# Softmax transposes taken from TensorE: through DRAM by GpSimd's queue, then VectorE

## The chip, the cores and the metric

The kernel runs on one core of one Trainium2 chip. The metric is the device time of one execution in microseconds. Runs of the kernel before took 885.91 to 886.01 us, with a median of 885.98 us (three runs).

The five engines of a core are TensorE (PE, with its weight loads as PEld), VectorE (DVE), ScalarE (ACT), GpSimd (POOL) and SyncE (SP), which in this kernel only issues DMAs. Each engine runs its own list of instructions in the order in which the program gave them to it, and waits at an instruction until what it needs is there.

## The reference

The program computes sliding-window attention, and two feed-forward layers on its output, all in float32:

```python
def _attn_ref(q, k, v):                      # each [4, 8, 576, 64]
    scores = scale * np.matmul(q, k.transpose(0, 1, 3, 2))
    rel = pos[:, None] - pos[None, :]
    mask = (rel >= 0) & (rel < 64)
    scores = np.where(mask, scores, -1000000000.0)
    scores = scores - np.max(scores, axis=-1, keepdims=True)
    attn = np.exp(scores)
    attn = attn / (np.sum(attn, axis=-1, keepdims=True) + 1e-09)
    return np.matmul(attn, v)

# layer 1, on x [2304, 512]: weights [512, 2048] and [2048, 512]
h = x @ w_in;  r = np.maximum(h, 0.0);  x = (r * r) @ w_out
# layer 2, same shapes
h = x @ w_in
P = a[0] + a[1] * h + a[2] * h**2 + a[3] * h**3
Q = 1.0 + abs(b[0]) * abs(h) + abs(b[1]) * h**2
out = (P / (Q + 1e-06)) @ w_out
```

## The kernel before

The 2304 tokens are cut into blocks of 512, 512, 512, 512 and 256. For each block of layer 1, sixteen steps j multiply a slice of the hidden layer (`h_mm`, L619: twelve matmuls of 128x512, three for each of four pieces of the inner dimension, because every float32 factor is split into a high and a low part of type float32r) and add its product into four accumulators in PSUM (`out_mm`, L638). Between the two, `mid1` applies the activation on ACT and DVE and ends with a subtraction on DVE (L692), which `out_mm` waits for. When a block ends, `evac1` copies the accumulators out (L705 to L707) to DRAM. These matmuls are the "big matmuls" of this text. Layer 2 does the same with `mid2` and L640.

The attention is computed for sub-blocks of 128 tokens, index i from 0 to 17. The first block's four sub-blocks stand ahead of everything. The sub-blocks of block n+1 are computed while PE works on layer 1 of block n, as short visits put between the big matmuls. A sub-block has these slots:

- `q` and `k`: the transposes of q and k. Up to index 11 PE does them; from 12 (`NPE`) on DVE does, as 32x32 transposes (L463, L485), of data that SP's DMAs have put through DRAM so that the 32x32 squares lie in the right places.
- `s` (`slot_s`): the scores, 16 small products in float32 (L525) into two PSUM banks, one for each half `gl` of the sub-block. `softmax` follows for each half: `top` on DVE (L542: mask, and the row's least negative score), `exp` on ACT (L547), `norm` and `mul` on DVE (L551 to L555), in a tile `sm` of 128 rows by 4x128 keys.
- `p` (`slot_p`), one for each half: PE transposes the four 128x128 parts of `sm` into a PSUM bank (L568), and ACT or DVE copies that to a tile `pT` (L573).
- `x` (`slot_x`): the values, 16 small products of `pT` with v (L585), whose result `split_x` splits into the high and low part of layer 1's input (L602, L603).
- `sx` (`slot_sx`): the scores of i and the values of i-1 in one visit of PE. Within a block all scores but the first are taken in this way.

While that goes on, `convert` (L399 to L419) also turns layer 2's weights into high and low parts on ACT and DVE, and SP moves them to DRAM.

The order of everything is made by a planner (class `Plan`): each piece of work is an item with the engines that could do it, a duration in ns, and a due time. `run` always takes the item that can start first, and among those the one that is due first, on a model of five resources ("pe", "act", "dve", "pool", "dma"). An item can start when those it depends on have ended plus a gap: 2000 ns after a DMA, 150 to 200 after most others. On the chip the planned times are gone: only each engine's order is left. `softmax`'s tiles take turns in a ring of two buffers (`sm0`, `sm1`); layer 2's `mid2` uses the same ring for its tile `ab`.

Of the kernel before, what the change touches and what calls it, by code (L numbers as in the profile page):

```python
# [9 lines left out]
F32 = mybir.dt.float32  # L10
F32R = mybir.dt.float32r
U32 = mybir.dt.uint32
ACTF = mybir.ActivationFunctionType
ALU = mybir.AluOpType
# [25 lines left out]
class Item:  # L40
    def __init__(self, engines, emit, due):
        self.engines, self.emit, self.due = engines, emit, due
        self.deps, self.users = {}, []
        self.end = None


class Plan:
# [42 lines left out]
    def run(self):  # L90
        for it in reversed(self.items):
            least = min(it.engines.values())
            for u in it.users:
                d = u.due - least - 150
                it.due = d if it.due is None else min(it.due, d)
            assert it.due is not None
        left = {it: len(it.deps) for it in self.items}
        free = dict.fromkeys(self.ENGINES, 0)
        open_ = {e: [] for e in self.ENGINES}
        order = []  # L100

        def opened(it):
            it.ready = {}
            for e in it.engines:
                it.ready[e] = max([d.end + self.gap(d.on, e) for d in it.deps], default=0)
                open_[e].append(it)

        for it in self.items:
            if not left[it]:
                opened(it)  # L110
        while len(order) < len(self.items):
            best = None
            for e in self.ENGINES:
                for it in open_[e]:
                    start = max(free[e], it.ready[e])
                    key = (start, it.due)
                    if best is None or key < best[0]:
                        best = (key, it, e)
            (start, _), it, e = best
            it.on, it.end = e, start + it.engines[e]  # L120
            free[e] = it.end
            for x in it.engines:
                open_[x].remove(it)
            order.append(it)
            for u in it.users:
                left[u] -= 1
                if not left[u]:
                    opened(u)
        for it in order:
            it.emit(it.on)  # L130
# [6 lines left out]
def dve(n, fast=False, ptr=0):  # L137
    return 68 + 1.042 * n / (2 if fast else 1) + 61 * ptr
# [3 lines left out]
def window_attention__moe_relu2__moe_rational_kernel(  # L142
# [21 lines left out]
    nc = tc.nc  # L164
# [8 lines left out]
    NSUB = NT // 128  # L173
    blocks = [(t0, min(512, NT - t0)) for t0 in range(0, NT, 512)]
    NB = len(blocks)
    orders = (list(range(NB)), list(range(NB - 2)) + [NB - 1, NB - 2])
    NS0 = blocks[0][1] // 128
    NPE = sum(n for _, n in blocks[:3]) // 128
    scale = 1.0 / float(D) ** 0.5

    ctx.enter_context(tc.manual_schedule())
    sb = ctx.enter_context(tc.tile_pool(name="sb", bufs=1))
    dram = ctx.enter_context(tc.tile_pool(name="dram", bufs=1, space=bass.MemoryType.DRAM))
    psum = ctx.enter_context(tc.tile_pool(name="psum", bufs=1, space=bass.MemoryType.PSUM))

    V, A, P, T = nc.vector, nc.scalar, nc.gpsimd, nc.tensor
    plan = Plan()
# [6 lines left out]
    SMALL = [("cb", 2), ("coef", 6), ("na", 4), ("b1", 1)] + [(f"{x}{i}", 4) for x in ("nm", "su", "rs") for i in range(4)]  # L194
    TAGS = ([("ident", [128, 128], F32), ("mask", [128, 2, 128], F32)] +
            [(f"kT{i}", [128, HP, W + 128], F32) for i in range(2)] + [(x, [128, n], F32) for x, n in SMALL] +
            [("pad", [128, 224], F32)] +
            [(f"wi{x}{j}", [128, DM], F32R) for j in range(NF) for x in "hl"] +
            [(f"wo{j}", [128, KT, 2, 2, 128], F32R) for j in range(NF // 2)] +
            [(f"x{x}{i}", [128, 4, KT, 128], F32R) for i in range(2) for x in "hl"] +  # L200
# [10 lines left out]
    mask = sb.tile([128, 2, 128], F32, tag="mask", name="mask")  # L211
# [19 lines left out]

    sq_d = {x: dram.tile([128, HP, (NSUB - NPE) * 4, 32], F32, name=f"{x}_squares_d") for x in "kq"}


    turn = {}

    def buf(place, shape, dtype=F32, pool=sb, view=None):

        if not isinstance(place, str):
            n = turn.get(place, 0)  # L240
            turn[place] = n + 1
            place = place[n % len(place)]

        def make():
            t = pool.tile(shape, dtype, tag=place, name=place)
            return view(t) if view else t

        return Buf(plan, place, make)

    def ring(name, n):  # L250
        return tuple(f"{name}{i}" for i in range(n))
# [3 lines left out]

    ALL_PS = ("t0", "h0", "t1", "h1", "acc0", "acc1", "acc2", "acc3")
    LD, RAW, CV = ring("ld", 6), ring("raw", 3), (0, 1, 2)
    KTP, QTP, SM, PT = ring("kT", 2), ring("qT", 2), ring("sm", 2), ring("pT", 2)
    shared = {}

    def part(place, tag, shape, dtype, view, gen=0):
# [51 lines left out]

    nat = {}

    def load(dst, pieces, size, slow=1, reads=(), due=None):
        def emit(_):
            for o, i in pieces():
                nc.sync.dma_start(out=o, in_=i)
        return plan.add({"dma": size / 360 * slow}, emit, reads, [dst], due)  # L320

    def toks(t0, n):
        done = 0
# [13 lines left out]
    def squares(nm, c, last, token):  # L337


        src = {"k": k, "q": q}[nm]  # L340
        pieces = list(toks(NPE * 128, NT - NPE * 128))
        b = sq_b[nm, c, last] = Buf(plan, f"{nm}_squares{c}{last}", None)
# [111 lines left out]
    def ps_buf():  # L454
        return buf(ps_places[0], [128, 512], F32, psum, cols(128))

    qT, kT, sm, pT = {}, {}, {}, {}
# [76 lines left out]
    def softmax(i, gl, ps):  # L534
        t = early(NF - 5 - i, gl, 128) if i < NS0 else buf(SM, [128, 4, 128])
        sm[i, gl] = t
        kind = int((2 * i + gl) % GPB == 0)
        nm, su, rs = (buf(ring(x, 4), [128, 4]) for x in ("nm", "su", "rs"))

        def top(_):  # L540
            for c in range(4):
                V.tensor_tensor_reduce(out=t.t[:, c, :], in0=ps.t[:, c, :], in1=mask[:, kind, :], scale=-scale,  # L542
                                       scalar=-NEG, op0=ALU.add, op1=ALU.min, accum_out=nm.t[:, c:c + 1])

        def exp(_):
            for c in range(4):
                A.activation(out=t.t[:, c, :], in_=t.t[:, c, :], func=ACTF.Exp, scale=-1.0, bias=nm.t[:, c:c + 1],  # L547
                             accum_out=su.t[:, c:c + 1])

        def norm(_):  # L550
            V.tensor_scalar(out=rs.t, in0=su.t, scalar1=1e-9, scalar2=None, op0=ALU.add)  # L551
            V.reciprocal(out=rs.t, in_=rs.t)

        def mul(e):
            (P if e == "pool" else V).tensor_tensor(out=t.t, in0=t.t, in1=rs.t.unsqueeze(2).to_broadcast([128, 4, 128]),  # L555
                                                    op=ALU.mult)

        plan.add({"dve": 850}, top, [ps], [t, nm])
        plan.add({"act": 1550}, exp, [nm, t], [t, su])
        plan.add({"dve": 350}, norm, [su], [rs])  # L560
        plan.add({"pool": 1400} if i < NS0 else {"dve": 690}, mul, [rs, t], [t])

    def slot_p(i, n, due):
        src, ps = sm[i, n], ps_buf()

        def tr(_):
            for c in range(4):
                T.transpose(ps.t[:, c, :], src.t[:, c, :], ident)  # L568

        plan.add({"pe": 430}, tr, [src], [ps], due)  # L570
        t = pT[i, n] = early(NF - 5 - i, 2 + n, 128) if i < NS0 else buf(PT, [128, 4, 128])
        plan.add({"act": act(512, True), "dve": dve(512)}, lambda e: (
            A.copy(out=t.t, in_=ps.t) if e == "act" else V.tensor_copy(t.t, ps.t)), [ps], [t])  # L573

    def slot_x(i, due, ps=None):
        joined = ps is not None
        ps = ps or ps_buf()
        vg = [nat["v", 2 * i + gl] for gl in range(2)]
        pt = [pT[i, n] for n in range(2)]

        def mm(_):
            for hp in range(HP):
                for gl in range(2):
                    for e in range(2):
                        T.matmul(  # L585
                            out=ps.t[e * 64:(e + 1) * 64, hp, gl * W:(gl + 1) * W],
                            lhsT=vg[gl].t[:, 2 * hp + e, :],
                            rhs=pt[gl].t[:, hp, (e ^ gl) * 64:((e ^ gl) + 1) * 64],
                            start=True, stop=True,
                        )  # L590

        if joined:
            return vg + pt, [ps], mm
        plan.add({"pe": 1250}, mm, vg + pt, [ps], due)
        split_x(i, ps)
# [173 lines left out]
    def slots_of(first, last):  # L769

        o = []
        for i in range(first, last):
            o += [("sx" if i > first else "s", i)]
            o += [("q", i + 1)] if i + 1 < NSUB else []
            o += [("p", i, 0)]
            o += [("k", i + 1)] if i + 1 < NSUB else []
            o += [("p", i, 1)]
        return o + [("x", last - 1)]
# [25 lines left out]
    for l in range(2):  # L804
# [4 lines left out]
        for s in range(len(steps) + 1):  # L809
            lag = LAGS[l][0] if s < len(steps) - NF else LAGS[l][1]  # L810
            if s < len(steps):
                bi, j = steps[s]
                due = due_h(l, bi, j)
                if l == 0 and j == 0 and bi + 1 < NB:
                    f = blocks[bi + 1][0] // 128
# [12 lines left out]
                hp = h_mm(l, bi, j, due)  # L828
                gs[s] = (mid1 if l == 0 else mid2)(bi, j, hp)
                if l == 0 and NF - 2 <= s < NF - 2 + 4 * HP:  # L830
                    z, c = divmod(s - NF + 2, 2 * HP)
# [11 lines left out]
            if l == 0 and s < len(steps):  # L843
                while slots and slots[0][1] < due_h(0, bi, j + 1):
                    x, d = slots.pop(0)
# [43 lines left out]
```

## Time and profile before

| | |
|---|---|
| median of 3 runs | 885.98 us |
| the profiled execution's own time | 890.21 us |
| its span in the profile | 888.4 us |
| TensorE's mean granted clock | 0.996 of full speed |
| TensorE busy | 870.5 us, 98% |
| VectorE busy | 674.3 us, 76% |
| ScalarE busy | 561.0 us, 63% |
| GpSimd busy | 11.5 us, 1% |
| DMA, moved in all | 113.64 MB |

The profile shows one execution, by the hardware's own profiler. "Busy" is the time in which an engine had an instruction in work. Matmuls overlap each other, so that PE's busy time says that it was never without work, and not that the work could not be done in less; where a visit's price is needed it is read from the starts of the matmuls around it. A wait is put down to the instruction that released it.

### The profile page before, as it was taken

Reading aid. Unit: us, or ns where it says so; the run is one execution under the profiler, and the core shown is the slowest. Engines: PE = TensorE matmul, PEld = TensorE weight load, DVE = VectorE, ACT = ScalarE, POOL = GpSimd, SP = SyncE. Lnnn points to the kernel's source line nnn. Section 1 sums busy time; section 2 is a strip of 40 time slices with the busy share of each in tenths; the row PEclk is TensorE's granted clock in tenths of the full one; section 3 lists DMA queues with packets and bytes.
Section 4 is the critical chain, followed back from the end, with each engine's and each line's share of the span. In section 5 each row is a group of like instructions: output and inputs, shape, how many; then the busy total and the mean of one; then the engine's idle time right before and its main releaser. Section 6 shows DMA issues by size and latency. Waiting matters only on the chain.

```text
span 888.4 us, 14088 instructions
## 1 busy us (share of the span) xinstructions
PE 870.5 (98%) x5152; PEld 726.5 (82%) x5152; DVE 674.3 (76%) x1435; ACT 561.0 (63%) x1172; POOL 11.5 (1%) x25
## 2 busy tenths in 40 slices
PE   7799999999999999999999999999999999999998
PEld 6678788888878888888899888888888888988886
DVE  6999995666466676754421899999999999999994
ACT  6778774656456554535444766676667667888764
POOL 4000000000000000000000000000000000000000
PEclk9999999999999999999999999999999999999999
DMA  9686662688855453633189910210011002100001
GB/s 230 187 243 199 188 192 84 200 219 220 223 179 184 147 184 141 238 134 126 49 313 372 361 45 0 96 48 1 1 47 48 1 1 94 49 1 24 1 1 48
DMA packets 152998, 113.64 MB, mean 128 GB/s; under 512 B 92769, under 2 KB 131681, under 8 KB 150881
## 3 DMA queue, kind: packets, MB, share of 16 engines
q1 hardware_dynamic: 152928, 112.75, 41.0%
q8 instruction: 40, 0.66, 0.3%
q14 instruction: 30, 0.24, 0.1%
HBM read 81.79 MB, written 34.08 MB: 130 GB/s over the span
## 4 chain that ended last, share of the span: by engine, by line
PE 88%; DVE 6%; DMA 3%; ACT 2%; issue 1%; SPq 0%; POOLq 0%; POOL 0%; ACTq 0%; DVEq 0%
PE h L619 30%; PE acc L640 22%; PE acc L638 19%; PE t L619 11%; PE t L525 1%; DMA raw<-in_moe_w_out_dram 1%; PE t L568 1%; DVE cvr L404 1%; PE h L585 1%; DVE cvr L407 1%; DVE sm L542 1%; DVE g L692 1%; DMA ld<-in_q_dram 0%; PE t L585 0%; DMA raw<-in_moe_w_in_dram 0%
## 5 line engine op out<-in xcount | busy, mean ns | idle before, releaser
L638 PE MATMUL acc<-g,wo 128*128 128x512 f32 (+1 forms) x960 | 215.9, 372 | 0.8 <-DVE g L692 0.8
L638 PEld LDWEIGHTS acc<-g,wo 128*128 128x128 f32 x960 | 167.3, 189 | 31.5 <-DVE g L692 1.4
L619 PE MATMUL h<-xh,wih 128*128 128x512 f32 (+1 forms) x480 | 181.1, 377 | 2.0 <-DVE rs L551 2.0
L619 PE MATMUL h<-xl,wih 128*128 128x512 f32 (+1 forms) x480 | 178.0, 371 | 0.3 <-DVE xl L603 0.3
L619 PE MATMUL h<-xh,wil 128*128 128x512 f32 (+1 forms) x480 | 178.3, 371 | 0.0
L619 PEld LDWEIGHTS h<-xh,wih 128*128 128x128 f32 x480 | 91.0, 190 | 18.0 <-ACT sm L547 2.1
L692 DVE TENSOR_TENSOR g<-cvr,g 128x512 fp32r<-128x512 f32 (+1 forms) x80 | 50.8, 635 | 71.7 <-ACT cvr L690 71.4
L619 PEld LDWEIGHTS h<-xh,wil 128*128 128x128 f32 x480 | 91.1, 190 | 16.0 <-DVE wil L419 0.4
L619 PEld LDWEIGHTS h<-xl,wih 128*128 128x128 f32 x480 | 91.1, 190 | 14.9 <-DVE xl L603 0.6
L685 ACT ACTIVATE cvr<-h 128x512 f32<-128x512 f32 (+1 forms) x80 | 44.3, 554 | 84.9 <-PE h L619 83.0
L640 PE MATMUL acc<-wo,cvr 128*128 128x512 f32 x384 | 93.1, 390 | 0.0
L640 PE MATMUL acc<-wo,g 128*128 128x512 f32 x384 | 93.1, 389 | 0.0
L640 PEld LDWEIGHTS acc<-wo,g 128*128 128x128 f32 x384 | 71.6, 188 | 14.6
L640 PEld LDWEIGHTS acc<-wo,cvr 128*128 128x128 f32 x384 | 71.5, 188 | 14.4
L736 DVE SCALAR_TENSOR_TENSOR kT<-kT,b,sm 128x512 f32<-128x512 f32 (+1 forms) x80 | 55.8, 698 | 16.4 <-ACT kT L731 13.8
L399 ACT ACTIVATE cvr<-raw 128x512 f32<-128x512 f32 x64 | 42.9, 671 | 30.3 <-DMA raw<-in_moe_w_out_dram 13.7
L738 ACT ACTIVATE raw<-kT,cb 128x512 f32<-128x512 f32 (+1 forms) x80 | 54.9, 686 | 8.8 <-DVE kT L736 6.6
L619 PE MATMUL t<-xl,wih 128*128 128x512 f32 (+1 forms) x160 | 58.9, 368 | 0.0
L619 PE MATMUL t<-xh,wil 128*128 128x512 f32 (+1 forms) x160 | 58.8, 368 | 0.0
L619 PE MATMUL t<-xh,wih 128*128 128x512 f32 (+1 forms) x160 | 58.8, 367 | 0.0
L749 DVE SCALAR_TENSOR_TENSOR pT<-pT,coef,raw 128x512 f32<-128x512 f32 (+1 forms) x80 | 55.8, 697 | 1.7
L740 ACT ACTIVATE raw<-raw,cb 128x512 f32<-128x512 f32 (+1 forms) x80 | 54.5, 681 | 1.7
(150 smaller groups left out, 1322.6 us busy)
## 6 DMA issues: line engine op xcount, KB each, us to landing
raw<-in_moe_w_in_dram SPq DMA_DIRECT2D x64, 256.0 KB, 3.4
raw<-in_moe_w_out_dram SPq DMA_DIRECT2D x32, 512.0 KB, 4.5
w2h_d<-raw SPq DMA_DIRECT2D x32, 256.0 KB, 2.1
w2l_d<-cvr SPq DMA_DIRECT2D x32, 256.0 KB, 2.1
ld<-in_v_dram SPq DMA_DIRECT2D x25, 256.0 KB, 3.9
out_dram<-ld SPq DMA_DIRECT2D x18, 256.0 KB, 2.1
x2h_d<-xh SPq DMA_DIRECT2D x4, 1024.0 KB, 5.1
x2l_d<-xl SPq DMA_DIRECT2D x4, 1024.0 KB, 7.7
```

What stands on the lines that cost most here:

```text
L399: plan.add({"act": act(DM)}, lambda e: A.activation(out=t.t, in_=raw.t.bitcast(F32)[:, :, 1], func=ACTF.Copy, scale=2.0 ** -112), [raw], [t])
L404: plan.add({"dve": dve(DM)}, lambda e: V.scalar_tensor_tensor(out=u(t), in0=u(t), scalar=3, in1=raw.t[:, :, 1], op0=ALU.logical_shift_left ...
L407: plan.add({"dve": dve(DM)}, lambda e: V.scalar_tensor_tensor(out=u(t), in0=raw.t[:, :, 0], scalar=29, in1=u(t), op0=ALU.logical_shift_rig ...
L619: T.matmul(out=v4(hp.t, n), lhsT=w.t[:, (c ^ 2) * 128:((c ^ 2) + 1) * 128], rhs=x.t[:, :n // 128, c, :], start=(c == 0 and z == 0), stop=( ...
L638: T.matmul(out=v4(acc[l, bi, m].t, n), lhsT=w.t[:, m, :], rhs=y.t[:, :n // 128, :], start=st, stop=en)
L640: T.matmul(out=v4(acc[l, bi, m].t, DM), lhsT=y.t[:, m, :], rhs=w.t, start=st, stop=en)
L685: plan.add({"act": act(n, True)}, lambda e: A.activation(out=r.t[:, :n], in_=hp.t[:, :n], func=ACTF.Relu), [hp], [r])
L692: plan.add({"dve": dve(n)}, lambda e: V.tensor_tensor(out=gl.t[:, :nq], in0=v4(r.t, n), in1=gh.t[:, :nq].bitcast(F32), op=ALU.subtract), [ ...
L736: plan.add({"dve": dve(n, ptr=1)}, lambda e: V.scalar_tensor_tensor(out=f(h2), in0=f(h2), scalar=b1, in1=f(ab), op0=ALU.mult, op1=ALU.add) ...
L738: plan.add({"act": act(n, ptr=1)}, lambda e: A.activation(out=f(y), in_=f(h2), func=ACTF.Ln, scale=2.0 ** -63, bias=cb[:, 0:1]), [h2], [y])
L740: plan.add({"act": act(n, ptr=1)}, lambda e: A.activation(out=f(y), in_=f(y), func=ACTF.Exp, scale=-1.0, bias=cb[:, 1:2]), [y], [y])
L749: plan.add({"dve": dve(n, ptr=1)}, lambda e: V.scalar_tensor_tensor(out=f(u), in0=f(u), scalar=coef[:, 0:1], in1=f(y), op0=ALU.subtract, o ...
```

## The change

From sub-block index 8 on (`NPD`, the tokens from 1024, that is, the ninth sub-block) three things change.

- `softmax` writes its tile in another order of columns: the 128 keys are cut into four runs of 32, and the four heads' runs of the same 32 keys stand together. `top`, `exp` and `mul` do the same work through such views. Behind `mul` two new items are put on GpSimd's DMA queue: one DMA writes the tile to DRAM (`p_d`), and four DMAs of 32 rows each read it back into the same tile with its 32x32 squares exchanged. `load` gets an argument `own` for that: the duration on "pool" that the planner is to reckon with, and a `lag` that stands in place of the gap behind it (700 and 5000 ns for the write, 2300 and 5000 ns for the four reads).
- `slot_p` is one 32x32 transpose on DVE of the whole tile into `pT`. No transposes on PE, no PSUM bank, no copy. `slot_x` reads its right operand from `pT` as two runs of 32 columns in place of one of 64.
- The slot `sx` is no longer used; `s` of i and `x` of i-1 are two visits, one behind the other in due time. `x` takes its PSUM bank from the attention's own two (`t0`, `t1`) in place of one of the big matmuls' (`h0`, `h1`).

The ring `sm` gets a third buffer, for all sub-blocks and for `ab` in layer 2.

```diff
         def opened(it):
             for e in it.engines:
-                it.ready[e] = max([d.end + self.gap(d.on, e) for d in it.deps], default=0)
+                it.ready[e] = max([d.end + (self.gap(d.on, e) if d.lag is None else d.lag) for d in it.deps],
+                                  default=0)
...
+    NPD = sum(n for _, n in blocks[:2]) // 128
...
-            [("pad", [128, 224], F32)] +
+            [("pad", [128, 208], F32)] + [("sm2", [128, 4, 128], F32)] +
...
+    p_d = dram.tile([NSUB - NPD, 2, 128, 4, 128], F32, name="p_d")
...
-    KTP, QTP, SM, PT = ring("kT", 2), ring("qT", 2), ring("sm", 2), ring("pT", 2)
+    KTP, QTP, SM, PT = ring("kT", 2), ring("qT", 2), ring("sm", 3), ring("pT", 2)
...
-    def load(dst, pieces, size, slow=1, reads=(), due=None):
+    def load(dst, pieces, size, slow=1, reads=(), due=None, own=None):
         def emit(_):
             for o, i in pieces():
-                nc.sync.dma_start(out=o, in_=i)
-        return plan.add({"dma": size / 360 * slow}, emit, reads, [dst], due)
+                (P if own else nc.sync).dma_start(out=o, in_=i)
+        it = plan.add({"pool": own[0]} if own else {"dma": size / 360 * slow}, emit, reads, [dst], due)
+        if own:
+            it.lag = own[1]
+        return it
...
+        if i >= NPD:
+            keys = lambda x: x.rearrange("p (k j) -> p k j", j=32)
+            head = lambda c: t.t.rearrange("p k (h j) -> p k h j", j=32)[:, :, c, :]
+            full = lambda: t.t.rearrange("p k (h j) -> p k h j", j=32)
+            sums = lambda: rs.t.unsqueeze(1).unsqueeze(3).to_broadcast([128, 4, 4, 32])
...
         plan.add({"pool": 1400} if i < NS0 else {"dve": 690}, mul, [rs, t], [t])
+        if i >= NPD:
+            d = p_d[i - NPD, gl]
+            b = Buf(plan, f"p_d{i}{gl}", None)
+            load(b, lambda: [(d, t.t)], 1 << 18, reads=[t], own=(700, 5000))
+            load(t, lambda: [(t.t[z * 32:(z + 1) * 32], d[:, z, :].rearrange("(a j) f -> j a f", j=32))
+                             for z in range(4)], 1 << 18, reads=[b], own=(2300, 5000))

     def slot_p(i, n, due):
-        src, ps = sm[i, n], ps_buf()
+        src = sm[i, n]
+        if i >= NPD:
+            t = pT[i, n] = buf(PT, [128, 4, 128])
+            plan.add({"dve": dve(512)}, lambda e: V.transpose(
+                t.t.rearrange("p a f -> p (a f)"), src.t.rearrange("p a f -> p (a f)")), [src], [t], due)
+            return
+        ps = ps_buf()
...
-                            rhs=pt[gl].t[:, hp, (e ^ gl) * 64:((e ^ gl) + 1) * 64],
+                            rhs=(pt[gl].t[:, (e ^ gl) * 2:(e ^ gl) * 2 + 2, hp * 32:(hp + 1) * 32] if i >= NPD else
+                                 pt[gl].t[:, hp, (e ^ gl) * 64:((e ^ gl) + 1) * 64]),
...
-            o += [("sx" if i > first else "s", i)]
+            o += ([("sx", i)] if first < i < NPD else [("s", i), ("x", i - 1)] if i > first else [("s", i)])
```

## Rows read from the trace of the kernel before

**Rows 1.** The page: busy time, share of the span, instructions of each engine.

```profile
PE 870.5 (98%) x5152; PEld 726.5 (82%) x5152; DVE 674.3 (76%) x1435; ACT 561.0 (63%) x1172; POOL 11.5 (1%) x25
```

**Rows 2.** Windows, 137 to 430 us: length, PE, PEld, DVE, ACT, POOL, clock, DMA, GB/s.

```profile
137.00:430.00 293.00, 290.83 (x1857) 237.43 (x1856) 182.81 (x465) 160.84 (x382) 0.00 (x0) 0.99 0.57 174
```

**Rows 3.** Waits of PE: line, releaser, us in total, times, longest.

```profile
PE t L568 <- DVE sm L555: 2.1, 1, 2.1
```

**Rows 4.** Timeline of PE: start us, length us, line, operation, count.

```profile
345.22 2.88 PE L638 MATMUL acc<-g,wo 128*128 128x512 f32 x12
347.94 0.39 PE L619 MATMUL h<-xh,wih 128*128 128x512 f32 x1
```

**Rows 5.** Line L568 (count, least, median, most ns, first and last start).

```profile
L568 PE MATMUL t<-ident,sm x112: 270/272/300, 39.1 to 416.0; 128*128 128x128 f32 x112
```

**Rows 6.** Timeline of PE around one transpose visit; nine big matmuls between.

```profile
407.66 0.60 PE L568 MATMUL t<-ident,sm 128*128 128x128 f32 x4
...
410.19 0.62 PE L638 MATMUL acc<-g,wo 128*128 128x512 f32 x2
```

**Rows 7.** Timeline of PE around a joined visit, scores alone, and values alone.

```profile
313.14 0.39 PE L619 MATMUL h<-xh,wil 128*128 128x512 f32 x1
313.46 1.10 PE L525 MATMUL t<-kT,qT 64*64 64x128 f32 x32
...
318.44 0.39 PE L619 MATMUL h<-xh,wih 128*128 128x512 f32 x1
...
245.21 0.39 PE L619 MATMUL h<-xh,wil 128*128 128x512 f32 x1
...
250.10 0.39 PE L619 MATMUL h<-xh,wih 128*128 128x512 f32 x1
...
425.42 0.39 PE L619 MATMUL h<-xh,wil 128*128 128x512 f32 x1
425.74 1.15 PE L585 MATMUL t<-pT,ld 128*64 128x64 f32 x32
...
428.32 0.61 PE L638 MATMUL acc<-g,wo 128*128 128x512 f32 x2
```

**Rows 8.** Line L463, DVE's transposes of q; then its wait, from all waits.

```profile
L463 DVE STREAM_TRANSPOSE qT<-ld x6: 706/711/712, 214.7 to 340.9; 128x512 f32<-128x512 f32 x6
...
DVE qT L463 <- DMA ld<-q_squares_d: 3.9, 3, 1.8
```

**Rows 9.** Line L319, 125 to 430 us: SP's issues in ns, and landing.

```profile
L319 SPq DMA_DIRECT2D w2h_d<-raw x31: 319/338/1339, 169.2 to 426.7; - x31
...
L319 SPq DMA_DIRECT2D ld<-q_squares_d x6: 529/530/590, 211.1 to 337.7; - x6
...
DMA to landing us min/median/max: 2.0/3.1/8.1
```

**Rows 10.** Timelines of DVE (first row) and PE, at the end of a block.

```profile
217.26 0.68 DVE L555 TENSOR_TENSOR sm<-sm,rs 128x512 f32<-128x512 f32 x1
...
231.98 1.15 PE L585 MATMUL t<-pT,ld 128*64 128x64 f32 x32
...
243.39 0.39 PE L619 MATMUL h<-xh,wih 128*128 128x512 f32 x1
```

**Rows 11.** Line L401 (count, least, median, most ns).

```profile
L401 DVE TENSOR_SCALAR raw<-raw x64: 400/424/433, 27.9 to 428.2; 128x512 uint32<-128x512 uint32 x64
```

**Rows 12.** Timeline of PE around the wait; then windows for that stretch.

```profile
255.76 0.63 PE L568 MATMUL t<-ident,sm 128*128 128x128 f32 x4 [2.10 <-DVE sm L555]
...
257.23 0.63 PE L619 MATMUL h<-xh,wih 128*128 128x512 f32 x1
257.65 0.63 PE L619 MATMUL h<-xl,wih 128*128 128x512 f32 x1
...
261.95 0.40 PE L619 MATMUL h<-xh,wih 128*128 128x512 f32 x1
...
253.60:262.00 8.40, 6.30 (x24) 5.09 (x24) 7.18 (x15) 4.96 (x13) 0.00 (x0) 0.80 0.45 187
```

More of the change, by code (lines that the diff above doesn't have):

```diff
@@ L44, in __init__ @@
         self.end = None
+        self.lag = None
 class Plan:
@@ L538, in softmax @@
         nm, su, rs = (buf(ring(x, 4), [128, 4]) for x in ("nm", "su", "rs"))
+        if i >= NPD:
[3 more added lines that the diff above has]
+            sums = lambda: rs.t.unsqueeze(1).unsqueeze(3).to_broadcast([128, 4, 4, 32])
+        else:
+            keys = lambda x: x
+            head = lambda c: t.t[:, c, :]
+            full = lambda: t.t
+            sums = lambda: rs.t.unsqueeze(2).to_broadcast([128, 4, 128])
         def top(_):
             for c in range(4):
-                V.tensor_tensor_reduce(out=t.t[:, c, :], in0=ps.t[:, c, :], in1=mask[:, kind, :], scale=-scale,
+                V.tensor_tensor_reduce(out=head(c), in0=keys(ps.t[:, c, :]), in1=keys(mask[:, kind, :]), scale=-scale,
                                        scalar=-NEG, op0=ALU.add, op1=ALU.min, accum_out=nm.t[:, c:c + 1])
@@ L546, in exp @@
             for c in range(4):
-                A.activation(out=t.t[:, c, :], in_=t.t[:, c, :], func=ACTF.Exp, scale=-1.0, bias=nm.t[:, c:c + 1],
+                A.activation(out=head(c), in_=head(c), func=ACTF.Exp, scale=-1.0, bias=nm.t[:, c:c + 1],
                              accum_out=su.t[:, c:c + 1])
@@ L554, in mul @@
         def mul(e):
-            (P if e == "pool" else V).tensor_tensor(out=t.t, in0=t.t, in1=rs.t.unsqueeze(2).to_broadcast([128, 4, 128]),
-                                                    op=ALU.mult)
+            (P if e == "pool" else V).tensor_tensor(out=full(), in0=full(), in1=sums(), op=ALU.mult)
         plan.add({"dve": 850}, top, [ps], [t, nm])
```

## The prediction

> **What bounds the kernel now.** I read the page's busy shares first. TensorE (PE) is busy 870.5 of 888.4 us; VectorE (DVE) has the next largest share, 76% [rows 1]. So the end is set by how much PE is given to do, plus its few waits. Next I read the stretch in which the changed sub-blocks are computed, 137 to 430 us: PE 290.8 of 293 us, DVE 182.8, ScalarE (ACT) 160.8, GpSimd (POOL) nothing, the DMA engines 57% [rows 2]. PE there has no slack and everyone else has. Third, PE's list of waits: the longest is one of 2.1 us, a softmax transpose (L568) waiting for DVE's last multiplication (L555) [rows 3]. Fourth, PE's timeline around each kind of attention visit, because a busy sum overstates overlapped matmuls: what a visit costs is how far it pushes the big matmuls behind it.
>
> **The pace.** Twelve undisturbed big matmuls take 345.22 to 347.94, or 2.72 us: 0.2267 us each [rows 4]. A visit's cost is the time between two big matmuls around it, less 0.2267 for each big matmul in it.
>
> **Removed: the softmax's transposes on PE.** From sub-block index 8 on (indices 8 to 17, ten of the eighteen) `slot_p` issues no PE work: two visits of four transposes each per sub-block, so 20 visits; their 80 transposes are part of the line's 112 [rows 5]. One visit: from its start at 407.66 to the big matmul at 410.19 are 2.53 us with nine big matmuls (2.04 us) in them, so 0.49 us [rows 6]. I measured four more visits in the same way: 0.47 to 0.50. Sum: 20 x 0.49 = **9.8 us off PE** (9.4 to 10.0). The copy that emptied PSUM behind each (L573, ACT or DVE) goes too; neither engine bounds this stretch, so I count nothing for it.
>
> **Split: scores and values.** Within a block, scores of i and values of i-1 were one visit; now they are two for i = 9, 10, 11, 13, 14, 15 and 17, seven times. The joined visit: 313.14 to 318.44 is 5.30 us with 13 big matmuls (2.95), so 2.35 us. Scores alone: 245.21 to 250.10 is 4.89 us with 16 (3.63), so 1.26; another one gave 1.30. Values alone: 425.42 to 428.32 is 2.90 us with 7 (1.59), so 1.31 [rows 7]. Split 1.28 + 1.31 = 2.59 against 2.35: 0.24 more, with bounds 0.20 to 0.28. Sum: 7 x 0.24 = **1.7 us onto PE**. Values now take their right operand as two runs of 32 floats in place of one run of 64. No row shows such an operand on PE. Below: nothing, since the count and shape of the matmuls stay. Above: I allow each of the 32 matmul records of a visit the price of a record again, 1.15/32 = 0.04 us, so 1.2 us x 10 sub-blocks = 12 us. I take nothing, because the weight loads between them are unchanged and pace these short matmuls. The 12 us end belongs to the slower cases below. The writes of `top`, `exp` and `mul` in runs of 32 floats also keep their element counts; nothing, since DVE and ACT have 38% and 45% of the stretch idle.
>
> **Added: DVE's transposes.** 20 of 128x512, at 0.71 us [rows 8], so 14.2 us on DVE, less the few copies that DVE did. That makes 197 of 293 us, 67%. It is hidden as long as PE's big matmuls do not wait for DVE; that cover is what the next part prices.
>
> **Added: the way through DRAM.** For each softmax tile, POOL issues one write of 256 KB and four reads of 64 KB: 100 DMAs in all, each waiting on POOL's own queue, which has nothing else to do in this stretch [rows 2]. SP's queue is not touched; POOL's is passed by no older work. No row shows a DMA issued by POOL. The nearest rows are SP's: 0.34 us to issue a 256 KB write, 0.53 to issue a read of the same size, and 2.0/3.1/8.1 us (least, median, most) from issue to landing [rows 9]. One tile alone: 0.34 + 3.1 + 4 x 0.53 + 3.1 = 8.7 us. The second tile of a sub-block is multiplied about 1 us after the first; its write has landed at 1.0 + 3.4, but the first tile's reads are issued until 3.4 + 2.1 = 5.6, so its own go from 5.6 to 7.7 and land at 10.8, which is 9.8 us after its multiplication. Bounds from the same rows: 0.34 + 2.0 + 2.1 + 2.0 = 6.4 us and 0.34 + 8.1 + 2.1 + 8.1 = 18.6 us. I take 9.8, since most landings are near the median.
>
> Against that stands what the plan allows. The diff gives the two loads 700 + 5000 and 2300 + 5000 ns, so the transpose is ordered on DVE about 13.0 us after the multiplication. DVE runs its instructions in that order. If the data lands in 9.8 us, the transpose finds it there. If it lands later, DVE stops, and what is behind it stops too: weight conversion (L401 to L419) and the subtraction (L692) that `out_mm` (L638) needs. How much of such a stop PE forgives has a row: in three of six cases the transposes of q already waited for their DMA, 3.9 us together, the longest 1.8 [rows 8]; PE's list of waits has nothing that follows from it. So 13.0 + 1.8 = 14.8 us from multiplication to landing cost PE nothing.
>
> The values visit needs both tiles. In the tightest place, the last sub-block of its block, the second multiplication ends at 217.9, the values began at 231.98, and the next block's big matmuls began at 243.39 [rows 10]. 217.9 + 9.8 + 0.7 = 228.4. That is before 231.98, and with values (1.3 us) and the split into high and low parts (about 1.3 us) there are still over 8 us to 243.39. With the 18.6 us case, and 2.1 more for the issues of the other tile, they are done by 242, just in time.
>
> The added bytes are 20 x 0.5 MB = 10.5 MB over 293 us, 36 GB/s on top of 174 [rows 2]. The DMA share rises from 57% to perhaps 65%, which SP's loads for the conversion bear while they stay ahead of ACT.
>
> A rule that speaks against this: DVE instructions of the kind of L401 can hold POOL up. The row: L401 takes 0.424 us, 64 times in the kernel [rows 11]. If every one of the five issues of a tile met one, that is 5 x 0.42 = 2.1 us, and 9.8 becomes 11.9 us, still under 13.0. The Trainium skill ("SBUF — State Buffer", section "SBUF: two separate sides") states that a DMA issued by GpSimd waits for its descriptors while VectorE runs an instruction that takes both SBUF ports, and gives about 620 ns alone and 3100 beside a copy. By that page's figures a tile would lose an estimated 5 x 2.5 = 12.4 us and every tile would be late. No run here shows it yet.
>
> **The third buffer** of the softmax ring lets scores of i+1 begin before both tiles of i are read back. The ring also serves the second layer's `ab`; PE is as full there, so nothing.
>
> **The one stall.** At 255.76 PE has waited 2.1 us, and from there to 261.95 it needs 6.19 us for a transpose visit (0.49) and 18 big matmuls (4.08): 1.6 us more, so 3.7 us lost. The 1.6 is the clock, granted at 0.80 in this stretch; big matmuls behind the wait start 0.43 us apart, the lower of the two levels, 1.2 GHz [rows 12]. The visit that waited is removed. But the reason is DVE emptying the accumulators of a finished block while a softmax runs, and `out_mm` stands seven instructions behind in PE's order and needs the same DVE's output. I take it that PE then waits there instead: gain 0, with 3.7 as the other end.
>
> **Sum.** -9.8 + 1.7 = -8.1 us. The profiled execution took 890.21 us (span 888.4 and 1.8 around it) and would take 882.1; the median of the runs shown is 4.2 below that execution, so by the same 8.1: **877.9 us**, 0.9% faster.
>
> **Rivals.**
> - *DVE waits for data that is late* (slower). Place: the DVE transpose, at the head of DVE's order. It costs from 14.8 us on. 2.1 us of waiting cost 3.7 with the clock [rows 12], so each us beyond is 1.8 us, ten times (the two tiles of a sub-block wait together): 18 us. The gain is gone at 0.45 us beyond, 15.3 us from multiplication to landing; at 1 us beyond the time is 877.9 + 18 = 895.9. For it: POOL's issue has no row, and single landings of 8.1 us. Against: the median sum is 9.8. The values' operand in two runs, if it cost its upper end, would also be here, at 890. By the Trainium skill's page named above this would be the outcome. Chance 0.17.
> - *The stall of 253 us goes as well*: 877.9 - 3.7 = 874.2. For it: the instruction that waited is gone. Against: the one behind it needs the same engine. Chance 0.10.
> - *The new order brings a stall of that kind elsewhere*, at one of the other block boundaries, where DVE has more to do than before: 877.9 + 3.7 = 881.6. Chance 0.13.
> - *PE's freed time is not used*: conversion, loads or ACT hold the matmuls to their old times and it stays at 886.0. Against: none of them is over 63% busy in the stretch. Chance 0.05.
> - The forecast, 877.9: 0.55. Its own range, from the bounds of its two terms and small waits, is 875.5 to 880.
>
> The range takes in all but the first rival: 873.0 to 887.0, with 0.83 of the chances. 0.2% is 1.8 us, about what a measurement of this kernel can tell from no change. Faster: 0.55 + 0.10 + 0.13 = 0.78. Same: 0.05. Slower: 0.17.
>
> **What would show it.** L568 with 32 transposes in place of 112 and no PE work on L573's PSUM tiles; 20 more DVE transposes of 0.71 us; values visits of about 1.3 us alone and 1.26 to 1.30 for scores; POOL's DMAs landing under 5 us, so that DVE's waits for the read-back tile are none or under 1.8 us; PE idle in this stretch no more than its 2.2 us of before. The prediction is wrong if DVE's waits name the read-back DMA with several us each and PE's waits for L692 grow with them, if the values visit is longer than 1.31 us, or if the granted clock falls in more places than the one.

## The result, and the profile after

The changed kernel took 892.01 us (median of six runs, 890.90 to 893.39), the kernel before 886.0 beside it: a ratio of 1.0056, 95% interval 1.0040 to 1.0071. It is slower by 0.56%, 5 us by the ratio (the two medians stand 6.0 us apart), where 0.9% faster was forecast. The profiled execution took 893.39 us, with a span of 891.1.

The page's busy shares of the changed kernel:

```profile
PE 864.7 (97%) x5072; PEld 719.7 (81%) x5072; DVE 682.7 (77%) x1452; ACT 551.0 (62%) x1155; POOL 67.8 (8%) x125
```

Its windows, the same stretch and columns as in [rows 2]:

```profile
137.00:430.00 293.00, 282.95 (x1765) 228.31 (x1763) 188.95 (x478) 148.33 (x360) 56.27 (x100) 0.99 0.71 208
```

PE has less to do (80 fewer matmul records over the whole span, [rows 1]) and needs longer. In the stretch it stands idle for 10.0 us of 293, where it was 2.2 [rows 2]. The DMA share went from 57% to 71%. The longest of what PE waited for from 137 to 440 us (line, releaser, us in total, times, longest):

```profile
PE t L615 <- DVE pT L591: 4.2, 4, 1.9
PE acc L669 <- DVE g L723: 2.4, 1, 2.4
PE t L480 <- DMA ld<-in_q_dram: 1.9, 1, 1.9
...
```

Before, there was one such wait of over 1 us, the one in [rows 3]; it is gone. The new ones are mostly for DVE: for the new transposes (L591) and for the subtraction that `out_mm` needs (L723, L692 before); one is for a load of q on SP's queue. So is DVE held up by tiles that come back late? The line of the new transposes, and all that its engine waited for, says no; nor did POOL's issues of the DMAs take long (ns: least, median, most):

```profile
L591 DVE STREAM_TRANSPOSE pT<-sm x20: 702/705/708, 162.2 to 417.6; 128x512 f32<-128x512 f32 x20
its engine sat idle before it (us, times) until:
who waited for it (us, times):
...
L325 POOL DMA_DIRECT2D sm<-p_d x80: 551/551/747, 151.8 to 410.9; - x80
...
L325 POOL DMA_DIRECT2D p_d<-sm x20: 559/563/744, 148.0 to 402.7; - x20
```

The list below "sat idle" is empty: no transpose stopped DVE. What did is seen in the timeline of the changed kernel ahead of the values of sub-block 11 (start us, us, engine, line, idle before it and releaser):

```profile
229.71 1.14 SPq L325 DMA_DIRECT2D raw<-in_moe_w_in_dram  x2
...
233.74 0.67 ACT L408 ACTIVATE cvr<-raw 128x512 f32<-128x512 f32 x1 [4.29 <-DMA raw<-in_moe_w_in_dram]
...
234.44 0.43 DVE L410 TENSOR_SCALAR raw<-raw 128x512 uint32<-128x512 uint32 x1 [4.26 <-ACT cvr L408]
...
235.52 0.70 DVE L591 STREAM_TRANSPOSE pT<-sm 128x512 f32<-128x512 f32 x1
...
238.09 0.70 DVE L591 STREAM_TRANSPOSE pT<-sm 128x512 f32<-128x512 f32 x1
238.85 0.86 PE L615 MATMUL t<-pT,ld 128*64 128x64 f32 x22 [1.53 <-DVE pT L591]
```

Read it from the top: SP issues the raw weights; ACT's first step of the conversion (L408) stands 4.29 us until they land; DVE's next step (L410) stands 4.26 us until ACT is done; the two transposes are behind it in DVE's order; and PE, in the middle of the values, waits for the second. The late data is not the softmax's. Here it is layer 2's weights, on SP's queue.

PE's longest wait, the one of 2.4 us, comes from another load on the same queue: DVE stands 3.76 us until the 32x32 squares of q land, and the subtraction that `out_mm` needs is behind that in its order.

```profile
223.85 0.71 DVE L472 STREAM_TRANSPOSE qT<-ld 128x512 f32<-128x512 f32 x1 [3.76 <-DMA ld<-q_squares_d]
224.49 0.65 DVE L723 TENSOR_TENSOR g<-cvr,g 128x512 fp32r<-128x512 f32 x1
...
225.19 4.37 PE L669 MATMUL acc<-g,wo 128*128 128x512 f32 x11 [2.36 <-DVE g L723]
```

ACT's waits for the raw weights in the stretch, first before, then after (us in total, times, longest):

```profile
ACT cvr L399 <- DMA raw<-in_moe_w_in_dram: 8.6, 6, 3.5
...
ACT cvr L399 <- DMA raw<-in_moe_w_out_dram: 7.8, 4, 4.4
```

```profile
ACT cvr L408 <- DMA raw<-in_moe_w_in_dram: 26.4, 11, 5.0
...
ACT cvr L408 <- DMA raw<-in_moe_w_out_dram: 24.0, 10, 5.6
```

16.4 us have become 50.4. That is a sighting in two kernels with different orders, though, and not yet a cause.

### The profile page after: what moved, and what is told of

Read it like the earlier page. It is cut to its first block, busy times and chain, and to the rows that moved or that the text cites. A ratio compares the mean times of both kernels' runs of the same rounds, so it can differ in the third digit from the quotient of the medians.

```text
span 891.1 us, 14166 instructions
## 1 busy us (share of the span) xinstructions
PE 864.7 (97%) x5072; PEld 719.7 (81%) x5072; DVE 682.7 (77%) x1452; ACT 551.0 (62%) x1155; POOL 67.8 (8%) x125
## 3 DMA queue, kind: packets, MB, share of 16 engines
q0 software_dynamic: 4160, 10.49, 3.9%
## 4 chain that ended last, share of the span: by engine, by line
PE 61%; DMA 3%; DVE 3%; issue 1%; SPq 1%; ACT 0%; DVEq 0%; ACTq 0%
PE acc L671 22%; PE h L650 19%; PE t L650 11%; PE acc L669 9%; DMA raw<-in_moe_w_in_dram 2%; DMA raw<-in_moe_w_out_dram 1%; SPq L325 1%; DVE sm L561 1%; DMA ld<-k_squares_d 0%; DVE pT L591 0%; PE t L615 0%; DMA w2h_d<-raw 0%; ACT cvr L408 0%; DVE g L723 0%; DVE sm L574 0%
## 5 line engine op out<-in xcount | busy, mean ns | idle before, releaser
L669 PE MATMUL acc<-g,wo 128*128 128x512 f32 (+1 forms) x960 | 217.7, 374 | 3.7 <-DVE g L723 3.7
L669 PEld LDWEIGHTS acc<-g,wo 128*128 128x128 f32 x960 | 169.0, 191 | 36.2 <-DVE g L723 5.0
L723 DVE TENSOR_TENSOR g<-cvr,g 128x512 fp32r<-128x512 f32 (+1 forms) x80 | 50.6, 632 | 68.9 <-ACT cvr L721 68.7
L408 ACT ACTIVATE cvr<-raw 128x512 f32<-128x512 f32 x64 | 42.7, 666 | 61.9 <-DMA raw<-in_moe_w_in_dram 30.1
L767 DVE SCALAR_TENSOR_TENSOR kT<-kT,b,sm 128x512 f32<-128x512 f32 (+1 forms) x80 | 55.7, 697 | 16.4 <-ACT kT L762 13.8
L410 DVE TENSOR_SCALAR raw<-raw 128x512 uint32<-128x512 uint32 x64 | 27.1, 425 | 44.7 <-ACT cvr L408 44.6
```

Source lines behind the costliest of these rows:

```text
L408: plan.add({"act": act(DM)}, lambda e: A.activation(out=t.t, in_=raw.t.bitcast(F32)[:, :, 1], func=ACTF.Copy, scale=2.0 ** -112), [raw], [t])
L410: plan.add({"dve": dve(DM, True)}, lambda e: V.tensor_scalar(out=raw.t[:, :, 1], in0=raw.t[:, :, 1], scalar1=0x80000000, scalar2=None, op0 ...
L669: T.matmul(out=v4(acc[l, bi, m].t, n), lhsT=w.t[:, m, :], rhs=y.t[:, :n // 128, :], start=st, stop=en)
L723: plan.add({"dve": dve(n)}, lambda e: V.tensor_tensor(out=gl.t[:, :nq], in0=v4(r.t, n), in1=gh.t[:, :nq].bitcast(F32), op=ALU.subtract), [ ...
L767: plan.add({"dve": dve(n, ptr=1)}, lambda e: V.scalar_tensor_tensor(out=f(h2), in0=f(h2), scalar=b1, in1=f(ab), op0=ALU.mult, op1=ALU.add) ...
```

## The experiments

Two theories went in. **A**: GpSimd's DMAs make SP's loads land late, and that goes through ACT and DVE to PE. **B**: the new order brings the stalls by itself. Each number is a ratio to the kernel before, run beside it on the same chip, with its 95% interval; us are medians.

**1. The order without the DMAs.**

```diff
-            for o, i in pieces():
-                (P if own else nc.sync).dma_start(out=o, in_=i)
+            for o, i in pieces() if not own else ():
+                nc.sync.dma_start(out=o, in_=i)
```

> The change with its 100 GpSimd DMAs left out; the planner still reckons with them, so the order on every other engine is that of the change (the transposes read the tile as it was multiplied, so the attention of sub-blocks 8 to 17 is another one). Theory A (the DMAs delay SP's loads: the weights that ACT's L408 waits for and the squares of q and k, and through ACT and DVE the matmuls): the stalls of the changed kernel between 187 and 340 us go, and the time is what TensorE's saved work gives, 885.98 - 8.1 = 877.9, or 874.2 if the old stall at 253 us stays away: 874 to 879. Theory B (the new order itself brings the stalls: transposes and values stand in places where DVE is late, whatever the DMAs do): 890 to 893, as the change.

881.59 us, 0.9942 (0.9919 to 0.9964): faster by 0.6%. From here to the change, in one and the same order on PE, DVE, ACT and SP, are 0.0114, 10 us: the price of the DMAs. B alone cannot be it. But 5 us saved are not the 8.1 of the sum; the profiled execution still shows 2.3 us of PE idle in the stretch, and ACT's waits for the raw weights are 23.3 us, where they were 16.4 in the old order and are 50.4 with the DMAs. So the new order does lose something without DMAs too.

**2. The DMAs without the change**, read back into a tile of their own, `scr0`:

```diff
...
+            load(b, lambda: [(d, t.t)], 1 << 18, reads=[t], own=(700, 5000))
+            load(u, lambda: [(u.t[z * 32:(z + 1) * 32], d[:, z, :].rearrange("(a j) f -> j a f", j=32))
+                             for z in range(4)], 1 << 18, reads=[b], due=10 ** 9, own=(2300, 5000))
...
```

> The kernel before, with the same 100 GpSimd DMAs added behind the multiplication, read back into a tile that nobody reads; the order on TensorE, VectorE, ScalarE and SyncE is that of before, and nothing waits for the new DMAs but the next user of a softmax buffer. Theory A: SP's loads land later and ACT waits longer at L399 and its like, so slower by about what the change lost against its saved work, 5 to 13 us: 891 to 899. Theory B: the DMAs alone cost nothing, 885 to 887.

894.90 us, 1.0085 (1.0067 to 1.0104). By the ratio 7.5 us slower, with nothing behind them that anyone uses, in the old order. DMA issues between 137 and 430 us, first before, then this run (KB each, median us from issue to landing):

```profile
raw<-in_moe_w_in_dram SPq DMA_DIRECT2D x32, 256.0 KB, 3.4
raw<-in_moe_w_out_dram SPq DMA_DIRECT2D x16, 512.0 KB, 4.5
w2h_d<-raw SPq DMA_DIRECT2D x31, 256.0 KB, 2.1
```

```profile
q0 software_dynamic: 4160, 10.49, 11.3%
...
raw<-in_moe_w_in_dram SPq DMA_DIRECT2D x32, 256.0 KB, 4.6
raw<-in_moe_w_out_dram SPq DMA_DIRECT2D x16, 512.0 KB, 5.3
w2h_d<-raw SPq DMA_DIRECT2D x30, 256.0 KB, 2.9
```

With the order the same, SP's DMAs in these rows land later by 0.8 to 1.2 us, and ACT's waits for the raw weights go from 16.4 to 34.9 us. The Trainium skill ("DMA: Bandwidth & Descriptors", section "Issuing engines are not separate DMA queues") says that DMAs started by the scalar, sync or gpsimd engine run on the same 16 DMA engines and interleave; the trace agrees in that SP's land later when GpSimd's run.

**3. and 4. Fewer DMAs, and the split alone.** The change without the reads (first edit), and the kernel before with scores and values apart from sub-block 9 on (second):

```diff
-            for o, i in pieces():
+            for o, i in pieces() if not own or own[0] == 700 else ():
```

```diff
-            o += [("sx" if i > first else "s", i)]
+            o += ([("sx", i)] if first < i < NPD else [("s", i), ("x", i - 1)] if i > first else [("s", i)])
```

> The change with the 80 reads left out and the 20 writes kept, so half of the bytes and a fifth of the DMAs (the attention of sub-blocks 8 to 17 is another one, as the tiles don't come back). Theory A by bytes: half of the loss, 882 to 886. Theory A by number of DMAs or by the reads into 32 rows: near the one without DMAs, under 881. Theory B: 890 to 893.

> The kernel before with scores and values as visits of their own from sub-block 9 on, and nothing else. By the visits' prices seven splits cost 1.7 us: 887 to 889. If it is slower than 890, the split has a price (a stall, a bank) that the visits' rows did not show, and theory B gains; A says nothing on it.

The write alone: 881.88 us, 0.9948 (0.9929 to 0.9967), as without any. The split alone: 888.0, 1.0009 (0.9998 to 1.0021), which holds the 1.7 us of the sum (0.2%).

**5. and 6. Bytes or pieces.** In place of the change's four reads, the same write again, or one read of the whole tile:

```diff
-            load(t, lambda: [(t.t[z * 32:(z + 1) * 32], d[:, z, :].rearrange("(a j) f -> j a f", j=32))
-                             for z in range(4)], 1 << 18, reads=[b], own=(2300, 5000))
+            load(t, lambda: [(d, t.t)], 1 << 18, reads=[b], own=(2300, 5000))   # or [(t.t, d)]
```

> The change with the four reads of each tile replaced by the same write once more, behind the first: as many bytes as in the change, 40 DMAs in place of 100, no DMA into SBUF, and the order of the change on the other engines (the tiles don't come back, so the attention of sub-blocks 8 to 17 is another one). If the loss goes with the bytes on the DMA engines: near the change, 889 to 893. If it goes with the reads, by their number or by their 32 rows at a time, or with waiting for them: near the run with one write, 880 to 883.

> The change with the four reads of 32 rows each as one read of all 128 rows, without the exchange of the squares: the same bytes and the same round trip, 40 DMAs in place of 100 (the attention of sub-blocks 8 to 17 is another one). If four DMAs into 32 rows each are what costs: 880 to 884. If bytes coming in through DRAM cost, however they are cut, or the wait for them: 889 to 893.

0.9985 (0.9969 to 1.0001) and 1.0013 (0.9993 to 1.0033): both between the ends. So from nothing to one write, two writes, write and read, write and four reads the ratios are 0.9942, 0.9948, 0.9985, 1.0013, 1.0056. One read of the same bytes costs less than four, so the way they are cut counts (20 reads in place of 80, and 3200 packets on GpSimd's queue in place of 4160). A second write costs what the first did not, but it adds bytes and DMAs at once, so that bytes alone are not shown to count. Neither guess was right alone; why four reads are worse than one was not followed further.

**7. Fewer sub-blocks**, from index 12 on:

```diff
-    NPD = sum(n for _, n in blocks[:2]) // 128
+    NPD = sum(n for _, n in blocks[:3]) // 128
```

> The change from sub-block index 12 on in place of 8, six sub-blocks in place of ten; scores and values stay joined before. Saved on TensorE: 12 transpose visits of 0.49 less 4 splits of 0.24, 4.9 us. If the loss comes mainly where the DMA engines are fullest (137 to 246 us, where SP also puts the squares of q and k through DRAM), this is faster than before by 2 to 5 us: 882 to 885 where the kernel before takes 887. If each sub-block's DMAs cost the same anywhere, six tenths of the change's loss stay: 888 to 891.

891.73 us, 1.0050 (1.0030 to 1.0071). Six tenths of the DMAs, all of them behind 257 us and so outside the fullest stretch, and as slow as the change. The loss is not a matter of the fullest stretch. Whether it is a price for each DMA this run can't tell: less is saved here as well (4.9 us in place of 8.1), so that the DMAs cost 4.4 + 4.9 = 9.3 us where all of them cost 5.0 + 8.1 = 13.1; six tenths of that would have given 890.8 us, which is inside the interval. The next runs decide it.

**8. The same DMAs in an order that expects them.** The change with one number of the planner changed:

```diff
         if a == "dma":
-            return 2000
+            return 4000
```

> The change with 4000 in place of 2000 ns in the planner's gap behind SP's DMAs: the work and the DMAs are the change's, only the order allows loads to land 2 us later. If the loss is ACT and VectorE standing in order before loads that land later than planned, most of it comes back: 878 to 884 where the kernel before takes 887. If the matmuls lose to something else (TensorE's visits themselves, bandwidth), it stays at 889 to 893.

883.66 us, 0.9954 (0.9937 to 0.9972): the change is now faster than the kernel before by 0.5%. Three runs tell where that comes from.

> The kernel before with the planner's gap of 4000 ns behind SP's DMAs, and nothing else. If the gap helps only because GpSimd's DMAs make loads late: within 2 us of the kernel before, 886 to 889. If the old order was too tight already: faster by 2 us or more, and then the gain of the change with the gap is smaller by as much.

> The kernel before with the gap of 4000 ns and with the 100 GpSimd DMAs that nobody reads; the order on TensorE, VectorE, ScalarE and SyncE is that of the kernel before with the gap. If the DMAs cost through loads that land later than the order allows: within 2 us of the kernel before with the gap, 886 to 890. If they cost by something that no order hides: 893 to 896, as without the gap.

> The change with the gap of 4000 ns and its 100 DMAs left out, in the order of the change with the gap (the attention of sub-blocks 8 to 17 is another one). If TensorE's saved work of 8.1 us is all there when no load is late: 878 to 881 where the kernel before takes 887. If part of it is lost to the order with or without DMAs (values behind transposes that stand late in VectorE's order): 881 to 883.

The kernel before with the gap: 1.0007 (0.9996 to 1.0018), so the gap is no gain by itself. With the useless DMAs as well, order unchanged: 1.0022 (1.0008 to 1.0036); what cost 7.5 us costs 1.3, though raw weights still land 5.1 and 5.9 us after their issue. So the same 100 DMAs have no fixed price; it depends on what stands in order behind the load that is late. And the change with the gap and without DMAs: 878.70 us, 0.9908 (0.9890 to 0.9926), 8.2 us faster. That is as much as TensorE's whole saved work.

**9. Joined again.** The change with the gap, and the joined slot back:

```diff
-            o += ([("sx", i)] if first < i < NPD else [("s", i), ("x", i - 1)] if i > first else [("s", i)])
+            o += [("sx" if i > first else "s", i)]
```

> The change with the gap of 4000 ns, and scores and values joined again in one visit (seven splits fewer). By the visits' prices 1.7 us less than the change with the gap: 880 to 883. If the joined visit must wait for tiles that come back late, its scores wait too and it is slower than the change with the gap: 885 or more.

886.93 us, 0.9999 (0.9981 to 1.0018), slower than with the split. The split costs 1.7 us by its visits and is worth it here. That a joined visit's scores wait for the tiles is the guess of the expectation, and it is not shown: PE waits for the new transposes only 0.2 us in this run, and it is DVE that waits 7.0 us for tiles that come back (3.4 with the split).

**10. Which loads.** The 4000 behind the raw weights only (the edit below, with the gap at 2000), and behind all but them (`.lag = 2000`, with the gap at 4000):

```diff
-        load(raw, src, 1 << 19, reads=token)
+        load(raw, src, 1 << 19, reads=token).lag = 4000
```

> The change, with 4000 ns reckoned behind the loads of the raw weights only (the ones that ACT's L408 waits for), 2000 behind SP's other DMAs. If the raw weights are the late loads that cost: near the change with the gap everywhere, 882 to 885 where the kernel before takes 887. If the squares, q, k and v are: near the change, 889 to 892.

> The counterpart: 4000 ns behind all of SP's DMAs except the loads of the raw weights, which keep 2000. If the raw weights are what costs: 888 to 892, as the change. If the others do: 882 to 885. If both share it, this and its counterpart both end between, 885 to 888.

0.9996 (0.9981 to 1.0011) and 1.0056 (1.0035 to 1.0078). The first gives about half back, the second nothing: the raw weights carry it. The profiled executions say where the other half of the first is. From the first `out_mm` of the second block (L638 before, L669 after) to that of the last block, the part of layer 1 beside which the changed sub-blocks run, are 297.2 us before, 299.7 in the change, 289.9 with the gap of 4000, 287.8 with 4000 behind the raw weights alone and 298.1 behind all but them. So there the raw weights give all of it. What the first lacks is lost ahead of this part, which begins at 154.4 us in it and at 150.0 with the gap everywhere; the first of GpSimd's DMAs is issued at 148.0 us in the change.

**11. More of it.** On top of the gap of 4000, later transposes and values; and a gap of 6000 instead:

```diff
-            load(b, lambda: [(d, t.t)], 1 << 18, reads=[t], own=(700, 5000))
+            load(b, lambda: [(d, t.t)], 1 << 18, reads=[t], own=(700, 7000))
...
-                             for z in range(4)], 1 << 18, reads=[b], own=(2300, 5000))
+                             for z in range(4)], 1 << 18, reads=[b], own=(2300, 7000))
```

```diff
-            return 2000
+            return 6000
```

> The change with the gap of 4000 ns, and 7000 in place of 5000 ns behind GpSimd's write and reads, so that transposes and values stand 4 us later in the order. If what is left of the loss is transposes or values waiting for tiles: 880 to 882. If the later values now collide with the end of a block: 884 to 888.

> The change with 6000 ns behind SP's DMAs. If what is left of the loss is loads that land even later than 4000 ns: 880 to 882. If the DMAs keep a price that no order hides, or if the conversion now falls behind: 883 to 887.

0.9980 (0.9965 to 0.9994) and 1.0051 (1.0033 to 1.0070): neither is better than 4000, and the second, clearly worse, looked like a price that no order hides. Its windows say otherwise:

```profile
30.00:137.00 107.00, 96.66 (x693) 75.76 (x683) 92.67 (x245) 73.43 (x185) 0.00 (x0) 0.97 0.68 185
137.00:430.00 293.00, 289.94 (x1783) 234.68 (x1782) 197.02 (x479) 156.25 (x363) 56.23 (x100) 1.00 0.72 213
```

The changed sub-blocks' stretch is nearly full. The loss is ahead of it: PE waits for the conversion of layer 1's weights (6.6 us in four waits), whose loads nothing disturbs and which now come too late in the order.

**12. Only where loads are late.** The change with the gap at 4000, layer 1's raw weights 2000 as before, and layer 2's 4000 or, in the second run, 6000 (the edit shown):

```diff
-        load(raw, src, 1 << 19, reads=token)
+        load(raw, src, 1 << 19, reads=token).lag = (2000, 6000)[l]
```

> The change with 4000 ns behind SP's DMAs, but 2000 as before behind the raw weights of layer 1, which are loaded before any GpSimd DMA runs. The first block's order is then nearer to that of the kernel before; expected 1 us under the change with 4000 everywhere, 881 to 884 where the kernel before takes 887. If the gap's gain came by chance of order, 886 to 890.

> The same with 6000 ns behind the raw weights of layer 2. If what is missing against the order without DMAs is raw weights that land later than 4000 ns: 879 to 882. If it is tiles that come back late, or a price that no order hides: 882 to 886.

885.78 us, 0.9988 (0.9977 to 0.9999), and 882.27, 0.9949 (0.9935 to 0.9963). The first is outside what was expected, and clear of the 0.9954 of 4000 everywhere, though only loads that no GpSimd DMA disturbs differ. Measured as in 10, the part beside the changed sub-blocks is no longer (287.5 us against 289.9), but it begins at 154.6 us in place of 150.0. So the order of the first block alone moves its end by 4 us, where executions of one order (the change, and 1, 3, 5 and 6) lie within 1.3 us, and that much of a ratio can be chance of order. It does not explain 10, whose two runs begin this part alike, at 154.4 and 154.9 us. The second's windows, and ACT's waits for the raw weights in the second of them:

```profile
30.00:137.00 107.00, 101.80 (x698) 82.15 (x699) 99.18 (x245) 80.75 (x186) 0.00 (x0) 0.95 0.72 202
137.00:430.00 293.00, 293.00 (x1830) 238.26 (x1830) 192.22 (x485) 156.15 (x373) 56.14 (x100) 1.00 0.72 212
```

```profile
ACT cvr L408 <- DMA raw<-in_moe_w_in_dram: 2.8, 1, 2.8
...
ACT cvr L408 <- DMA raw<-in_moe_w_out_dram: 1.0, 1, 1.0
```

All 100 DMAs run, the DMA share is 72%, and PE is busy for 293.00 of 293 us. The part from block to block, measured as in 10, takes 284.7 us, where the run of 8.2 us without DMAs needs 286.1. So these traces show no price of the DMAs in this stretch that an order cannot hide; what they cost is lateness. Against the 8.2 us of the order without DMAs some 4 are still missing, and not in this stretch: it begins at 154.3 us in place of 150.1, and the first block's windows show a granted clock of 0.95, where the run of 8.2 us had 1.00 there. This version and the change with 4000 everywhere both beat the kernel before and the change; between the two the intervals do not decide.

## Why the prediction was wrong

- **Right: PE's saved work.** The sum was -8.1 us; the order without DMAs and with the gap measured -8.2. That the two agree so closely is in part luck, since the order ahead moves the time by 4 us on its own. The part measured in 10, with the gap and PE never idle in the stretch, is 293.8 us in the kernel before and 286.1 in the change without DMAs: 7.7 less. The visits' prices, read off as pushes of the matmuls behind, held: values alone cost 1.30 us in the changed trace (428.64 to 430.85 with four big matmuls), so the two-run operand costs nothing, and L568's 112 transposes are 32.
- **Right: no transpose waits for its tile.** DVE's list of waits ahead of L591 is empty. Landing took longer than the rows of SP said, 4.0 us for a write and 5.9 for a read, and stayed inside the 13 us that the plan allows. The slower rival had the right engine and the wrong releaser: its place, the transpose, was not where DVE stopped in the change. In some later orders it is: 10.2 us in five waits in the last run of 12, and PE is still never idle in that stretch.
- **Wrong: the step "which SP's loads for the conversion bear while they stay ahead of ACT".** The prediction counted the added bytes, 57% to 65% of the DMA engines (71% measured), and priced them at nothing, because nobody would wait. The cover was not there: ACT already waited 16.4 us for the raw weights in that stretch, a row that the waits of the kernel before hold and that the prediction does not use. A load that ACT already waits for has no slack: with the order unchanged, later landing made these waits 34.9 us. From ACT it went on to DVE and PE. The squares of q on the same queue came late too: DVE's longest wait for them is 3.8 us, 1.3 in the same order without the DMAs, and it stands behind PE's longest wait. The term has a size now: 10 us (1.0056 less 0.9942), 7.5 in the old order.
- **Wrong: the form of the slower rival's price**, a threshold for each sub-block times ten. The same 100 DMAs cost 7.5 us in the old order and 1.3 in the order with the gap; the loss is made where a late load, ACT's order and DVE's order meet ahead of something that PE needs at once.
- **The stall of [rows 12]** did go, as one rival said; no run shows what that alone gave.
- The granted clock fell in two new places in the changed trace, behind waits of 2.4 and 1.9 us, as [rows 12] had shown that it does.

Open: why four reads of 32 rows cost more than one read of the same bytes, and why the first block's order moves the time by 4 us, with the lower clock there in the order that is full in the stretch.

## What to carry to other kernels

A transfer added on an idle queue is not free because its own consumer has time; ask which transfers on other queues are already waited for, and read that list of waits before the DMA share. Where the order is fixed ahead by a planner's latencies, traffic that makes loads land later has to go into these latencies; behind loads that it does not disturb, a longer latency cost time here at 6000 ns and not at 4000. The cheapest test of such a change is to run its order without its transfers and its transfers without its order: here the first was 5 us faster and the second 7.5 slower, inside a result of 5 us slower. And a new order can move the time by some us where nothing was changed, so compare the stretch concerned as well as the whole.

## What the runs showed of the hardware that was not expected

- 10.5 MB more through GpSimd's queue over 293 us (36 GB/s on 174) moved the median landing of SP's 256 KB stores from 2.1 to 2.9 us and of the 256 KB weight loads from 3.4 to 4.6, in the same order and with the DMA engines at 69%.
- GpSimd's issue of one of these DMAs took 0.55 us at the median and 0.75 at most among 100, while VectorE was busy 64% of the time. The Trainium skill ("SBUF — State Buffer", section "SBUF: two separate sides") gives about 620 ns for a DMA of GpSimd alone and 3100 beside a VectorE copy, from which the prediction estimated 2.5 us more for each issue; here no issue came near that.
